# A new task order for a recurrent attention block with a gelu MLP behind it

## The chip, the cores and the metric

The kernel runs on one core of a Trainium2 chip. A core has five engines that run their own instruction lists and wait for each other by semaphores: TensorE (PE, matrix products into PSUM), VectorE (DVE), ScalarE (ACT), GpSimd (POOL) and SyncE (SP), which here does nothing but issue DMA transfers. The metric is the device time of one execution in microseconds (us).

## The reference

Two blocks follow each other, both in 32-bit floats. The first is a linear recurrence with a 40 by 40 state for each of 4 batches and 8 heads, over 768 steps:

```python
for t in range(S):
    y[:, :, t] = np.einsum('bhd,bhde->bhe', rt, state)
    Sa = np.einsum('bhde,bhe->bhd', state, at)
    state_decay = state * wt[:, :, None, :] - np.einsum('bhd,bhe->bhde', Sa, bt)
    state = state_decay + np.einsum('bhd,bhe->bhde', vt, kt)
```

The second takes the result as 3072 tokens of 320 numbers and runs them through an MLP of width 2048:

```python
h = x @ w_in
g = h * (1.0 / (1.0 + np.exp(-1.702 * h)))
return (g @ w_out).astype(np.float32)
```

## The kernel before, in words

The 768 steps are cut into 12 chunks of 64, and a chunk into two units of two batches each, so there are 24 units; unit i belongs to chunk i // 2 and needs the state that unit i - 2 left. Inside a unit the recurrence is written as products of 64 by 64 matrices for each head, and a triangular system that five "levels" of products invert. When both units of a chunk are done, the chunk's 256 tokens go through the MLP.

The work of a unit, by the names of its PSUM tiles and the lines of the code:

- `decay` (L536): the logarithms of w, their sums (`ps_cum`, `ps_cumc`; from unit 4 on a scan on DVE), and the exponentials FT, GT and G on ACT (L565 to L591).
- `prep` (L613): products of a, b and k with the exponentials (ahT L619, bhT L621, khT L624, kh and bh L627), the scores `ps_A` and `ps_RV` and their masks (L638, L650).
- `inverse` (L660): the score `ps_N`, its copies (P21 L692, E0 L689), then the levels. In the first four units a level is `ps_level` on PE, a copy of its result (PV, L784) and a transpose (EX, L723). In the others it is `ps_level`, a copy W (L751), a difference E (L753), a transpose ES (L702) and a spread over four diagonal blocks, EX (L707 on ACT, L709 on POOL or DVE). Then T0, Tc (L797), `ps_Q`, QT, `ps_T` and T (L830).
- `solve` (L835): the state read (`ps_zT`, `ps_rz`), the known part (`ps_B`, copies L891), the solution (`ps_X`, masked to M at L907), the result (`ps_y`), the new state (zraw, L934), the output read-out (L943) and its product with FT (x, L953). SP then writes x to DRAM (L963) and reads it back in another layout (xT, L967).
- `mlp` (L974): for a chunk 40 tasks "up" (`ps_up`, 64x256 products), four gelus on ACT (L988), and 16 tasks "down" (`ps_down`, 64x320 products), then a copy and an addition (L1012, L1014) and the store (L1011).

The weights come as eight pieces of four loads each, and each piece is then rebuilt from two words by ACT (L447), three DVE steps (L451 to L459) and POOL (L463). The first two pieces are needed by the first up, the fifth by the first down.

Nothing of this is scheduled when the kernel is built. `Plan.add` gathers 2700 tasks in a fixed sequence, with what each reads and which buffer must be free. `ORDER` is a text with one word per task: its number in that sequence, a letter for the engine (p PE, a ACT, d DVE, g POOL, s SP), and for tasks that touch PSUM a digit, which of the four pairs of PSUM banks the tile takes. `Plan.listed` reads the words, and the tasks are issued in that order; each engine thus takes its own tasks in the order of the text and waits, in place, for whatever a task needs:

```python
for one in text.split():
    e = next(e for e in ENGINES if ENGINES[e] in one)
    n, bank = one.split(ENGINES[e])
    t = self.tasks[int(n)]
    assert e in t.engines and t.after <= done and (e == "SP" or (t.pair is None) == (not bank))
    t.engine, t.bank = e, int(bank or 0)
```

`t.engines` names the engines on which a task may run: a W copy may be on ACT or DVE, a spread on ACT, DVE or POOL. Two tasks that read one PSUM pair on two engines take turns in the order of the text. SP is one such list as well: a load that waits for a free buffer holds up every transfer behind it.

Some numbers that come up again: 3a is the logarithm of unit 0; 103p and 159p are `ps_N` of units 0 and 1; 107, 110, 113, 116 and 119 are the levels of unit 0 (L0, L2, L4, L6, L8), 163, 166, 169, 172 and 175 those of unit 1 (L1, L3, L5, L7, L9); 292, 295, 298, 301, 304 and 362, 365, 368, 371, 374 the levels of units 2 and 3 (L10 to L19, even ones of unit 2); 136p and 192p are `ps_y` of units 0 and 1; 195 is x of unit 1 and 196s, 197s its way out to DRAM and back; 198p to 218p are the first ups; 19a is the first step of rebuilding weight piece 0; 2629p is `ps_y` of the last unit and 2634p the first up of the last chunk. In names like N(1) or M(0) the number is that of the unit.

Of the kernel before, what the change touches and what calls it, by code (L numbers as in the profile page):

```python
# [107 lines left out]
0s 8s 26s 5s 7s 9s 3a 6s 87p0 88p1 24s 89a1 1s 2s 12s 102a 95d 100p2 90a0 93d 158a 101d2 98p3 96g 10s 94d 17s 97g 16s 99d3  # L108
103p1 4a 11s 132p0 104a1 105d1 142p2 143p3 133a0 106d 130p1 14s 144a3 13s 107p0 15s 18s 151g 108a0 109d0 51s 131a1 110p3 27s
149g 150d 111a3 112d3 159p0 156p1 145a2 161d0 160a0 152g 113p3 345s 92a 162d 25s 153d 114a3 163p2 42s 115d3 34s 19a 274s 264p0  # L110
165d2 265p3 164a2 22d 266a3 166p2 20d 273s 21d 33s 43s 167a2 154p3 168d2 23g 35s 28a 157d1 116p2 155d3 169p1 117a2 118d2 267a0
279d 63s 280g 119p3 277s 171d1 36s 44s 123a3 120d3 343s 125d3 121a 278g 124d3 29d 287a 126p2 170a1 288p0 127a2 30d 172p1 479s
122a3 31d 289a0 128p2 54s 173a1 45s 129d2 32g 62s 174d1 134p3 37a 290d0 175p2 344s 135d3 180a2 146s 178a2 275s 176d2 136p1
179a2 38d 181a2 39d 177a 282g 276s 291d 91s 138a1 182p0 188p3 281d 183a0 186p2 139d 137a1 283p0 187a2 184p1 189a3 40d 140s
292p2 46a 60s 284d0 41g 285p3 185d1 148a 286d3 190p0 293a2 294d2 334p1 335p3 357a 191d0 141s 268g 147s 336a3 315d 192p2 47d
337a1 348d 316p0 194a2 346s 295p3 349d 61s 317a0 195g 347s 358p1 296a3 297d3 360d1 318a0 298p3 271a 361d 319p0 338g 300d3 196s
193a2 320a0 355p2 385d 270s 48d 299a3 362p0 356d2 351g 301p3 363a0 364d0 350g 386p2 197s 302d3 365p0 387a2 269s 352g 359a1
303d3 388a2 323p1 367d0 366a0 321p3 49d 324a1 304p2 322a3 478s 325d1 50g 353p0 309a2 470p3 354d0 209p1 307a2 210p1 310a2 305d2
211p1 308a2 272d 198p0 341a 199p0 72s 212p1 70s 64a 200p0 340s 368p2 52s 342d 339s 69s 201p0 369a2 202p0 370d2 203p0 471a
213p1 65d 214p1 389p2 66d 472a3 483g 204p0 390a2 560s 371p3 67d 306a 53s 215p1 71s 482s 216p1 372a3 217p1 476a 220p2 373d3 68g  # L120
218p1 221p2 477d 219a1 205p0 222p2 206p0 223p2 224p2 78s 559s 207p0 55a 311p3 225p2 79s 312d3 80s 226p2 208a0 58d 313p1 374p3
314d1 227p2 56d 379a3 228p2 229p2 57d 326p0 230a2 59g 393p1 327d0 378a3 391p2 394a1 375d3 231p0 558s 392d2 376a 232p0 233p0
395d1 81s 73a 234p0 480s 381p2 235p0 474s 328p1 475s 382a2 74d 377a3 485d 380a3 236p0 75d 481s 492a 242p2 486d 243p2 82a 76d
484d 77g 383p3 237p0 384d3 244p2 329d1 330d1 488p3 473d 238p0 531d 245p2 487g 246p2 489d3 85d 532p1 708s 239p0 533a1 396p3
331d 534a1 240p0 247p2 397d3 332s 241a0 562s 535p1 83d 490p3 536a1 84d 398p0 706s 572a 491d3 86g 550p1 253p3 399d0 551a 555s
400d0 561s 333s 254p3 401d 255p3 552a1 564d 493p0 402s 556a 567g 570p1 554s 494d0 248p2 705s 563d 566g 249p2 495d0 498d 256p3
571d1 565g 403s 250a2 496a0 251d2 696p1 497g 557d 539p0 252s 537p2 257p3 538a2 704s 540d0 701s 258p3 553d 611d 697a 499d 573p2
259p3 576a2 574d2 784s 710d 700s 260p3 787s 541d0 575d2 404p0 578d 261a3 577g 405p0 579d 698a1 568p2 711g 500p1 406p0 569d2
501a1 407p0 262d3 580p2 702a 502d1 263s 408p0 582d2 409p0 503d 410p0 583d 504a 612p3 411p0 584g 613d3 412p0 614d3 413p0 505p1
709d 414a0 426p3 506d1 427p3 428p3 507d1 429p3 699d 581d2 430p3 615p1 703d 431p3 616a1 785s 585p0 432p3 508d 586a0 433p3 587d0  # L130
434p3 509a 588d 435p3 589d 448p2 436a3 510p1 590p0 511a1 449p2 592d0 591a0 512d1 415p3 513d 416p3 593d 514a 417p3 594g 418p3
515p0 419p3 516a0 517d0 595p1 518d 420p3 596a1 597d1 421p3 598d 422p3 519a 599d 423p3 424p3 520p0 425a3 437p1 521d0 438p1
523d0 522g 439p1 524d0 440p1 525d0 441p1 442p1 526d0 527p3 718p0 528a3 443p1 719d0 929s 444p1 720d0 529p3 445p1 721d0 446p1
530d3 600p0 723d 447a1 542p3 722d 724g 603d0 605a0 619p1 604d0 543d3 450p2 620a1 606d0 544p3 621d1 601d0 602d 617p1 707s 546d3
451p2 618a1 783s 712d 547g 713d 607p0 725p1 608a0 452p2 609p0 453p2 548s 610d0 932s 454p2 727d1 726d1 622p0 728d 545d3 729a
775p1 455p2 623d0 780s 776a 549s 756d 730p3 624p0 456d2 457d2 731d3 458s 459p2 777a1 778g 732d3 786s 788g 781a 779s 626d0
460p2 625d0 627g 733d 795p1 835d 734a 461p2 735p3 791g 462p2 628s 736a3 796d1 737d3 716p0 792g 738d 463p2 782d 739g 1011s
920p1 757p3 925s 464p2 717d0 758a3 629s 759a3 790d 465p2 740p0 789d 466p2 741a0 742d0 921a 797p3 467d2 760p0 1008s 468d2 800a3
923d 652p2 469s 761d0 922a1 653p2 926a 930s 798d3 714p1 799d3 654p2 924s 802d 801g 655p2 934d 803a 656p2 836p0 657p2 715d1
658p2 659p2 837d0 762p3 838d0 927d 660p2 763a3 661p2 764p1 662a2 743d 630p0 744d 928s 631p0 632p0 765d1 804p3 766d1 633p0  # L140
805a3 806d3 634p0 807d 635p0 808a 745p2 636p0 748d2 637p0 749d2 839p1 933g 750d2 638p0 840a1 1009s 751d2 639p0 809p3 746d2
935g 640a0 641p1 810d3 642p1 793p2 747a 811d3 674p0 812d 794d2 813a 752p3 643p1 753a3 814p2 644p1 815a2 816d2 754p3 645p1
755d3 646p1 817d 647p1 818a 767p2 841p3 768d2 648p1 842a3 649p1 819p2 650p1 820a2 821d2 769p3 822d 651a1 823d 675p0 771d3 931s
770d3 772g 824p2 936d 676p0 827a2 828a2 942p1 829a2 677p0 1153s 830a2 937d 945a1 773s 663p3 825d2 664p3 943d1 1156s 826a 665p3
944d1 999p2 947d 946g 666p3 1000a 1004s 980d 940p1 948g 667p3 941d1 668p3 774s 669p3 670p3 831p1 671p3 1001a2 1002d 1003s
832d1 672p3 1005a 1013d 678p0 673a3 1006d 833p2 843p1 679p0 834d2 1007s 844d1 938p2 845d1 680p0 939d2 846p3 681p0 847d3 949p1
1012g 682d0 848p2 950a1 683d0 1014d 684s 685p3 849d2 1015g 1010s 850d2 1021p0 1016g 951d1 686p3 1024a0 1232s 851d 1235s 981p2
687p3 982a2 952d 852s 1022d0 983a2 953g 1144p1 1023d0 688p3 1026d 1145a 1149s 1025d 1027g 984p2 1059d 689p3 1154s 954p0 853s
985a2 1147g 690p3 1158d 1148s 955a0 956d0 986p2 1146a1 957d 1150a 691p3 958d 987a2 1151d 988p0 692p3 989a0 1152s 990d0 959p1
693a3 865p2 960a1 694d3 866p2 961d1 867p2 695s 962d 868p2 963d 1028p0 869p2 1029a0 1030d0 870p2 1031d 1157g 871p2 1159d 1032a  # L150
1060p3 872p2 873p2 1061a3 874p2 1062d3 1033p1 875a2 854p0 1035d1 855p0 1036d 856p0 1037d 1063p3 857p0 1064d3 1034a1 858p0
964p2 859p0 965a2 966d2 1038p1 967d 860p0 1039a1 1040d1 861p0 1041d 1017p3 968a 1042g 862p0 1018d3 863p0 969p2 864a0 876p1
970d2 877p1 972d2 971g 1043p3 973d2 878p1 1044a3 974d2 879p1 975d2 880p1 881p1 1045d3 1019p0 1046d 976p2 1047a 882p1 1020d0
1233s 883p1 977a2 1166p3 884p1 1169a3 1167d3 1377s 978p0 885p1 1168d3 898p2 1171d 1170g 886a1 979d0 887p3 1172a 1048p0 991p1
1051a0 888p3 1052a0 992d1 889p3 1053a0 890p3 1054a0 891p3 1049d0 993p1 1050a 1067p0 994d1 1160g 1155s 892p3 1161d 1068a0 893p3
894p3 1069d0 1380s 895p3 1204d 1065p0 995d1 896p3 996d 1066a0 1231s 1055p1 899p2 897a3 1056d1 997s 1173p0 1223p3 900p2 1174a0
1175d0 1228s 1176d 1224a 1177g 1057p1 901p2 1058d1 1070p0 998s 1164p1 1225a3 1226d 1236g 1227s 1071d0 902p2 1229a 1165d1
1162p3 903p2 1238d 1163d3 904p2 1237d 1178p0 1230d 905p2 1179a0 1180d0 1245p1 906a2 1181d 1072p3 1248a1 1456s 907d2 1182g
1246d1 908s 1247d1 909p0 1250d 1234s 1239g 1073d3 1251a 910p0 1240g 1074d3 1249d 1183p2 1459s 1283d 1368p1 911p0 1184a2 1075d
1373s 912p0 1185d2 1369a 1076s 1186d 1252p3 1187d 913p0 1370a1 1371g 1372s 1382d 1253a3 1188p2 1254d3 1374a 914p0 1255d 1190d2  # L160
1256g 1077s 1189a2 1191d 1243p1 1375d 915p0 1192g 1257p3 916p0 1244d1 1258a3 1259d3 1205p2 917d0 1206a2 1193p1 918d0 1207a2
# [968 lines left out]
```

## Time and profile before

| | |
|---|---|
| median of three runs | 679.86 us (679.8, 679.86, 681.62) |
| span of the profiled execution | 681.1 us |
| PE busy | 652.0 us (96%) |
| DVE busy | 445.5 us (65%) |
| ACT busy | 330.7 us (49%) |
| POOL busy | 176.7 us (26%) |
| `ps_up` matmuls | 254.4 us busy, 31% of the chain that ended last |
| `ps_down` matmuls | 240.3 us busy, 30% of that chain |
| `ps_level` matmuls | 9% of that chain |
| moved by DMA | 69.73 MB, 102 GB/s over the span |

The times of the three runs are of whole executions; the span is that of the one execution that the hardware profiler recorded, from its first instruction to its last. In a row such as `L751 ACT COPY W<-ps_level 128x512 f32 x56 | 32.7, 585 | 69.1 <-PE ...` one reads: line, engine, operation, output and input with their shapes, how many; busy time in us and the mean of one in ns; the idle time just before them and what ended it. A matmul of 32-bit floats appears twice in the records, and four of them run side by side on quarters of the array, so a matmul's own duration is much longer than the interval at which they follow each other. PEclk is the granted clock of TensorE as a share of full speed.

### The profile page before, as it was taken

How to read it: one execution, taken by the hardware profiler on the slowest of the kernel's cores; microseconds unless marked ns; L12 is line 12 of the kernel's file. 1: busy time of each engine (PE TensorE's matmuls, PEld its weight loads, DVE VectorE, ACT ScalarE, POOL GpSimd, SP SyncE). 2: the span in 40 equal slices, each digit the busy share in tenths (PEclk: the TensorE clock that was granted, in tenths of full speed). 3: DMA queues.
4: the chain of work that ended last, by engine and by line, in shares of the span. 5: the costliest groups of instructions: out<-in, count | busy, mean ns of one | idle time of the engine just before them, and what ended most of it. 6: DMA issues, size and time to landing. Idle time of an engine off the chain costs nothing.

```text
span 681.1 us, 42181 instructions
## 1 busy us (share of the span) xinstructions
PE 652.0 (96%) x19488; PEld 572.4 (84%) x19488; DVE 445.5 (65%) x906; ACT 330.7 (49%) x688; POOL 176.7 (26%) x204
## 2 busy tenths in 40 slices
PE   5777999999999999999999999999999999999997
PEld 5667888997987788888888898899899799889996
DVE  4687877777867668767776587868556766675001
ACT  4675845544564654664545445455454354252110
POOL 5443444225123123123123211321412421300000
PEclk9788999999999999999999999999999999999999
DMA  7874755205314314432404413513502312200100
GB/s 235 275 244 148 228 158 173 89 14 155 108 50 139 103 45 125 124 108 67 121 23 131 140 34 107 154 33 106 149 29 71 121 51 58 58 13 23 51 12 21
DMA packets 35312, 69.73 MB, mean 102 GB/s; under 512 B 5440, under 2 KB 14656, under 8 KB 35136
## 3 DMA queue, kind: packets, MB, share of 16 engines
q1 hardware_dynamic: 35136, 67.03, 32.8%
q8 instruction: 153, 2.51, 1.6%
q14 instruction: 23, 0.19, 0.1%
HBM read 59.15 MB, written 7.86 MB: 98 GB/s over the span
## 4 chain that ended last, share of the span: by engine, by line
PE 91%; DMA 4%; ACT 1%; DVE 1%; issue 1%; SPq 0%; ACTq 0%; DVEq 0%
PE ps_up L300 31%; PE ps_down L300 30%; PE ps_level L300 9%; PE ps_y L300 5%; PE ps_B L300 4%; PE ps_X L300 2%; PE ps_N L300 2%; PE ps_rz L300 2%; PE ps_RV L300 2%; PE ps_A L300 1%; DMA ak<-in_ak 1%; PE ps_zT L300 1%; PE ps_Q L300 1%; DMA time<-in_time 1%; PE ps_T L300 1%
## 5 line engine op out<-in xcount | busy, mean ns | idle before, releaser
L300 PE MATMUL ps_up<-xT_all,w_sb 64*64 64x256 f32 x3840 | 254.4, 377 | 2.0 <-DMA xT_all<-x_dram 1.1
L300 PE MATMUL ps_down<-w_sb,g 64*64 64x320 f32 x3072 | 240.3, 430 | 1.1 <-issue 0.9
L300 PEld LDWEIGHTS ps_up<-xT_all,w_sb 64*64 64x64 f32 x3840 | 172.9, 133 | 17.7 <-issue 2.5
L300 PEld LDWEIGHTS ps_down<-w_sb,g 64*64 64x64 f32 x3072 | 143.3, 133 | 31.4 <-issue 1.6
L988 ACT ACTIVATE g<-ps_up 128x1024 f32<-128x1024 f32 x48 | 49.1, 1024 | 44.7 <-PE ps_up L300 44.3
L709 POOL TENSOR_TENSOR EX<-ES,quads 128x512 f32<-128x512 f32 x29 | 38.3, 1323 | 115.5 <-DVE ES L702 83.1
L751 ACT COPY W<-ps_level 128x512 f32<-128x512 f32 x56 | 32.7, 585 | 69.1 <-PE ps_level L300 67.4
L300 PEld LDWEIGHTS ps_level<-W,EX 64*64 64x64 f32 x2560 | 59.2, 134 | 5.8 <-DVE T L830 0.2
L300 PE MATMUL ps_level<-W,EX 64*64 64x64 f32 (+1 forms) x2560 | 56.2, 217 | 0.0
L753 DVE TENSOR_TENSOR E<-two,ps_level 128x256 f32<-128x256 f32 x80 | 33.1, 415 | 34.7 <-ACT W L751 30.7
L707 ACT ACTIVATE EX<-ES,quads 128x256 f32<-128x256 f32 x80 | 36.3, 501 | 30.4 <-DVE ES L702 29.9
L619 POOL TENSOR_TENSOR ak<-ak,FT 128x512 f32<-128x512 f32 x16 | 22.0, 1378 | 76.2 <-DMA ak<-in_ak 54.4
L300 PE MATMUL ps_level<-PT,EX 64*64 64x64 f32 (+2 forms) x1280 | 34.9, 244 | 5.7 <-DVE EX L723 4.8
L300 PEld LDWEIGHTS ps_level<-PT,EX 64*64 64x64 f32 x1280 | 32.6, 145 | 8.9 <-DVE EX L723 5.7
L702 DVE STREAM_TRANSPOSE ES<-E 128x256 f32<-128x256 f32 x80 | 35.2, 442 | 4.7 <-DVE E L753 0.5
L300 PE MATMUL ps_y<-M,bh 64*64 64x104 f32 (+1 forms) x768 | 34.8, 247 | 1.3 <-DVE M L907 0.8
L300 PE MATMUL ps_y<-RV,kh 64*64 64x104 f32 (+1 forms) x768 | 34.9, 247 | 0.3 <-DVE EX L723 0.3
L891 ACT COPY B<-ps_B 128x416 f32<-128x416 f32 (+1 forms) x34 | 16.5, 492 | 33.5 <-PE ps_B L300 33.2
L300 PEld LDWEIGHTS ps_y<-RV,kh 64*64 64x64 f32 x768 | 28.9, 133 | 2.0 <-DVE M L907 0.5
L907 DVE TENSOR_TENSOR M<-ps_X,later 128x832 f32<-128x832 f32 (+1 forms) x24 | 23.8, 993 | 9.8 <-PE ps_X L300 9.5
L627 POOL TENSOR_TENSOR kh<-time,G 128x320 f32<-128x320 f32 x18 | 16.2, 902 | 48.4 <-PE ps_y L300 34.4
L300 PEld LDWEIGHTS ps_y<-M,bh 64*64 64x64 f32 x768 | 27.0, 133 | 1.9 <-DVE M L907 1.2
(131 smaller groups left out, 1097.2 us busy)
## 6 DMA issues: line engine op xcount, KB each, us to landing
ak<-in_ak SPq DMA_DIRECT2D x48, 160.0 KB
rv<-in_rv SPq DMA_DIRECT2D x48, 160.0 KB
time<-in_time SPq DMA_DIRECT2D x24, 320.0 KB
xT_all<-x_dram SPq DMA_DIRECT2D x48, 160.0 KB
wc<-in_wc SPq DMA_DIRECT2D x20, 264.0 KB
logw<-in_w SPq DMA_DIRECT2D x24, 160.0 KB
RV<-in_v SPq DMA_DIRECT2D x24, 160.0 KB
b<-in_b SPq DMA_DIRECT2D x48, 80.0 KB
```

Source lines behind the costliest of these rows:

```text
L300: nc.tensor.matmul(o, lhsT, rhs, start=start, stop=True, skip_group_check=True)
L619: plan.add(R, {"DVE": 690.0, "POOL": 1270.0, "sbuf": True}, lambda t: of(t.engine).tensor_mul(ahT(), ahT(), FT_of(i)), reads=T("ak", "FT") ...
L627: plan.add(R + 4, {"POOL": 870.0, "DVE": 490.0, "sbuf": True}, lambda t, n=n, dst=dst: of(t.engine).tensor_mul(dst(i)[:, :, :D], by_head(t ...
L702: plan.add(rank, dve(256), lambda t: nc.vector.transpose(ES(n), source(t)), writes=[key("ES", n, 6)], **reads)
L707: nc.scalar.activation(dst[:, :, h], ES(n), ACT.Copy, scale=quads[:, h, :1])
L709: of(t.engine).tensor_mul(dst, ES(n).unsqueeze(2).to_broadcast([128, 8, 2, 32]), quads.unsqueeze(1).to_broadcast([128, 8, 2, 32]))
L751: plan.add(rank, any2(512), lambda t: copy(t.engine)(tiles_of(W(n + 1)), blocks(psum(t, ""), 64)), writes=[key("W", n + 1, 5)], pair=pair)
L753: plan.add(rank, dve(256), lambda t: nc.vector.tensor_sub(tiles_of(E(n + 1)), every(two32, [128, 2, 4, 32]), blocks(psum(t, ""), 64)[:, :, ...
L891: plan.add(R, any2(4 * wide), lambda t: copy(t.engine)(dst(), some(psum(t, "")[:, :, :208])), writes=[("Bv", i)] if x and c > 0 else T("B" ...
L907: plan.add(R + 1, dve(8 * wide), lambda t: nc.vector.tensor_tensor(M_of(i)[:, :, :wide].rearrange("p (j b) n -> p b j n", b=2), some(psum( ...
L988: plan.add(-45, {"ACT": 1030.0, "table": "gelu"}, lambda t: nc.scalar.activation(g_of(c * NQ + q).rearrange("p m r n -> p r m n"), psum(t, ...
```

## The change

The text `ORDER` is replaced by another; nothing else in the kernel differs. All 2700 tasks are there as before, and each does the same arithmetic. The new text was found by a search on an estimate that lets the packets that bring the instructions queue behind the loads on the DMA engines. It changes three things: the order of the tasks on each engine, the engine of the tasks that have a choice, and the PSUM pairs.

```diff
 ORDER = """
-0s 8s 26s 5s 7s 9s 3a 6s 87p0 88p1 24s 89a1 1s 2s 12s 102a 95d 100p2 90a0 93d 158a 101d2 98p3 96g 10s 94d 17s 97g 16s 99d3
-103p1 4a 11s 132p0 104a1 105d1 142p2 143p3 133a0 106d 130p1 14s 144a3 13s 107p0 15s 18s 151g 108a0 109d0 51s 131a1 110p3 27s
...
+0s 7s 26s 102a 1s 5s 11s 100p0 3a 88p1 158a 8s 6s 9s 4a 51s 87p2 89a1 12s 95d 93d 17s 94d 103p1 105d1 101d0 98p3 90a2 96g 97g
+10s 2s 143p2 16s 104a1 99d3 142p0 106d 13s 132p3 133d3 107p1 15s 144a2 24s 130p2 109d1 151g 131d2 108a1 92a 110p1 149g 150d
...
-2468p0 2630d2 2559s 2469p0 2631d 2470p0 2632s 2471p0 2475p1 2472a0 2473d0 2476p1 2474s 2633s 2477p1 2478p1 2479p1 2480p1
-2634p3 2635p3 2636p3 2637p3 2638p3 2639p3 2640p3 2641p3 2642p3 2643p3 2481p1 2644a3 2482p1 2645p2 2483a1 2646p2 2484d1 2678p0
...
+2475p2 2628d3 2476p2 2629p3 2630d3 2477p2 2474s 2478p2 2558s 2559s 2479p2 2480p2 2631d 2632s 2481p2 2482p2 2633s 2634p3 2645p1
+2635p3 2636p3 2637p3 2638p3 2646p1 2647p1 2648p1 2649p1 2639p3 2640p3 2641p3 2483d2 2484d2 2485s 2642p3 2643p3 2650p1 2651p1
...
 """
```

How many tasks with a choice stand on which engine (those with a change of three or more):

| task | before | after |
|---|---|---|
| W copy, L751 | ACT 56, DVE 24 | ACT 38, DVE 42 |
| EX spread, L707 and L709 | ACT 40, DVE 31, POOL 29 | ACT 34, DVE 44, POOL 22 |
| T0 spread | ACT 13, DVE 5, POOL 6 | ACT 9, DVE 12, POOL 3 |
| B copies, L891 | ACT 34, DVE 14 | ACT 21, DVE 27 |
| P21 copy, L692 | ACT 22, DVE 2 | ACT 12, DVE 12 |
| QT, L816 | ACT 18, DVE 6 | ACT 13, DVE 11 |
| Tc copy, L797 | ACT 44, DVE 52 | ACT 54, DVE 42 |
| kh, L627 | DVE 6, POOL 18 | DVE 11, POOL 13 |
| ahT, L619 | DVE 8, POOL 16 | DVE 11, POOL 13 |
| khT, L624 | DVE 12, POOL 12 | DVE 7, POOL 17 |
| wz, L595 | DVE 12, POOL 10 | DVE 7, POOL 15 |
| W0 difference, L697 | DVE 9, POOL 11 | DVE 12, POOL 8 |
| zT copy, L858 | ACT 25, DVE 19 | ACT 29, DVE 15 |
| last copy of the output, L1012 | ACT 15, DVE 9 | ACT 12, DVE 12 |

ACT switches between its exponential and its gelu table 25 times in the new text, 29 times in the old one. PE waits for semaphores in 237 instructions of their own, 293 before. Between `ps_y` of the last unit and the first up of the last chunk stand six downs of the chunk before, where there were ten.

More of the change, by code (lines that the diff above doesn't have):

```diff
@@ L243 @@
[L243 to L244 removed]
+0s 7s 26s 102a 1s 5s 11s 100p0 3a 88p1 158a 8s 6s 9s 4a 51s 87p2 89a1 12s 95d 93d 17s 94d 103p1 105d1 101d0 98p3 90a2 96g 97g
+10s 2s 143p2 16s 104a1 99d3 142p0 106d 13s 132p3 133d3 107p1 15s 144a2 24s 130p2 109d1 151g 131d2 108a1 92a 110p1 149g 150d
+159p2 112d1 111a1 156p3 14s 145a0 161d2 162d 160d2 113p1 115d1 114d1 163p0 164a0 153g 265p2 152d 264p1 18s 19a 165d0 20d 266a2
@@ new lines @@
+2122g 2139p2 2179d 2076d0 2146d 1972s 1973s 2265a 2278d 2269s 2124s 1809p1 1810p1 1811p1 2145d 2147g 2075d0 2140d2 2106p2
+2268s 2148p0 2267g 2266a3 2270a 2149a0 2271d 1974p3 1975p3 1976p3 1977p3 1978p3 2107a2 1979p3 2150d0 2077d 2108p2 1980p3
+2180p0 2181a0 2078g 2182a0 1981p3 2109d2 2151d 2152d 1982p3 2272s 1983p3 2137p0 1812p1 2110d2 2138d0 1985p2 2353s 1813d1
+2153p0 1986p2 1984a3 1987p2 1814d1 2154d0 2079p1 2155d0 2156d 2080d1 2183p3 2157d 2184a3 2351s 2277g 1988p2 2081d1 2082d
+2018p0 1989p2 2158p1 2083d 1990p2 1991p2 2160d1 2279g 2161d 2084p3 1992p2 2085a3 2159d1 1993p2 2086d3 2087d 1994p2 1996p1
@@ new lines @@
+2038d2 2209p2 2303p0 2304d0 2305d0 2496d 2210p2 2370p1 2211p2 2039s 2201p3 2306d 2307d 2372d1 2212p2 2373d 2202p3 2203p3
+2204p3 2374a 2308p0 2310d0 2205p3 2309a0 2489d 2206p3 2371d1 2207p3 2213p2 2311d 2359p1 2375p0 2312g 2208a3 2377d0 2376a0
+2378d 2379a 2360d1 2497d 2214p2 2215p2 2216p2 2217p2 2218p2 2220p1 2221p1 2380p0 2382d0 2222p1 2219a2 2383d 2223p1 2405p2
+2313p3 2406d2 2381a0 2384a 2224p1 2314d3 2225p1 2319a3 2566s 2226p1 2385p2 2227p1 2228p1 2387d2 2386d2 2315g 2320p0 2229p1
+2321d0 2504p2 2317d3 2230a1 2388d 2389g 2318d3 2316a3 2505d2 2507d2 2242p0 2243p0 2506d2 2231p2 2508g 2232p2 2322p3 2323d3
```

255 lines of the change are left out of this document (122 added, 133 removed).

## The prediction

> **What bounds the kernel now.** I read the page's busy line and its slices first, then busy time by stretch, then the PE intervals and the instruction queue's packets, then the chain of waits, last the operation groups.
>
> ```profile
> PE 652.0 (96%) x19488; PEld 572.4 (84%) x19488; DVE 445.5 (65%) x906; ACT 330.7 (49%) x688; POOL 176.7 (26%) x204
> PE   5777999999999999999999999999999999999997
> PEclk9788999999999999999999999999999999999999
> DMA  7874755205314314432404413513502312200100
> q8 instruction: 153, 2.51, 1.6%
> ```
>
> TensorE is busy everywhere but in the first six slices and the last. The next rows, busy time by stretch, show the head: DMA is 0.77 to 0.84 busy for 51 us, PE works 64 of the first 85 us, and its granted clock falls to 0.80.
>
> ```profile
> core 0: us, PE busy (x) PEld busy (x) DVE busy (x) ACT busy (x) POOL busy (x), PEclk, DMA share, GB/s
> 0.00:17.00 17.00, 9.48 (x248) 8.56 (x248) 7.90 (x14) 6.99 (x25) 9.91 (x42) 1.00 0.80 235
> 17.00:34.00 17.00, 12.10 (x412) 10.90 (x416) 10.86 (x16) 10.46 (x21) 8.03 (x6) 0.80 0.84 275
> 34.00:51.00 17.00, 12.53 (x489) 11.25 (x486) 14.26 (x28) 13.14 (x33) 7.48 (x4) 0.90 0.77 244
> 51.00:68.00 17.00, 13.24 (x542) 12.16 (x532) 12.44 (x18) 9.71 (x25) 6.47 (x11) 0.90 0.49 149
> 85.00:102.00 17.00, 15.60 (x414) 13.76 (x408) 12.12 (x23) 7.85 (x18) 7.12 (x3) 1.00 0.52 159
> ```
>
> Busy time of overlapping matmuls hides short waits, so I took, for every PE task, the interval to the next task's first matmul, and each kind's median (up 0.432 us, down 1.077, y 1.427, a solver level 0.465, or 1.10 with W beside it). The medians of all 1080 tasks sum to 640.9 us. First task 3.75, last task starts 674.83: so 30.2 us are waits, 26.6 before 102 us and 3.6 after; 6.3 us follow (last down, store). Work does not change, so the new order can move only these waits. The first up starts at 69.0 us after 40.9 us of work: 28.1 us lost there.
>
> Some waits belong to the instruction stream. 39272 PE instructions came in 153 packets of 16384 bytes, one per 256 instructions. At each 256th, the next packet is requested (its start follows by a median 0.68 us, 2 to 3 us under loads, and it takes 0.88 to 1.76), and PE does not pass the following boundary until 1.3 to 1.5 us after the landing, wherever it stands still there. The chain of waits shows it as "issue":
>
> ```profile
> 54.25 0.56 issue
> 58.98 0.85 issue
> 70.94 0.19 issue
> 89.77 0.48 issue
> 95.04 0.92 issue
> ```
>
> At these boundaries PE's instructions stood still for 0.76, 1.06, 0.57, 0.86 and 1.34 us; later for 0.70 (196 us), 0.43 (557) and 0.28 (611). With one at 67 us (0.29) that is 6.3 us.
>
> **The change.** It moves every task, so I cost it by stage. The price rows of moved work:
>
> ```profile
> L751 DVE COPY W<-ps_level 128x512 f32<-128x512 f32 x24 | 16.3, 681 | 7.9 <-PE ps_level L300 7.6
> L751 ACT COPY W<-ps_level 128x512 f32<-128x512 f32 x56 | 32.7, 585 | 69.1 <-PE ps_level L300 67.4
> L709 DVE TENSOR_TENSOR EX<-ES,quads 128x512 f32<-128x512 f32 x31 | 21.7, 699 | 1.0
> L707 ACT ACTIVATE EX<-ES,quads 128x256 f32<-128x256 f32 x80 | 36.3, 501 | 30.4 <-DVE ES L702 29.9
> ```
>
> Task counts by these durations: DVE from 452 to 492 us (18 W copies at 0.68, 13 spreads at 0.70, B, P21, T0 copies), ACT 342 to 306 (four table loads at 1.28 fewer among it), POOL 163 to 146. Beside 641 us of PE work all three stay hidden on average. Where not, it shows in one of four terms.
>
> *Head, to the first up.* I followed the new lists by hand: each engine takes its tasks in order, a task begins 0.05 us after its last input or predecessor, two engines reading one PSUM pair take turns in list order (as L723 waits for L784's copy now), loads land by their place in SP's queue at the measured 0.27 MB/us. Before in brackets. ak(1) has 3.44 MB up to it (3.11), so lands near 17.9 (16.7); b(1) is early; both POOL products follow (1.38, 1.28) and N(1) starts 20.5 (20.67). Unit 0's lead of half a microsecond is lost behind N(1) on PE: L4 22.3 (22.46), L3 27.65 (27.80). Then weight 0's rebase (1.40) stands behind unit 1's level copy on ACT, not before it: L5 31.45 (31.56). L7 comes at 35.55 (37.61), since DVE takes EX7 before three masks and bhT(2). M(0) 40.65 (41.71). Unit 1's last transpose goes ahead of the Tc copies, so its T0 spread starts 42.15 (44.57); T(1) 46.95 (49.02); M(1) 49.15 (51.44); y(1) ends 51.9 (53.78). x(1) on POOL runs 52.75 to 54.7; 2.5 us out and 3.4 back make xT 60.6. Meanwhile L11 58.6 (61.27), L16 60.75 (63.03), L13 62.35 (64.92), and the first up, whose xT then waits already, at 63.2 (69.0). SP blocks twice, at RV(2) until y(0) and at RV(3) until y(1); what is queued behind, ak(3) and xT(0)'s first half, has 7 us to spare. PE has 38.7 us of work before the first up (40.9). So waits fall from 28.1 to 24.5: -3.6. The other bound: DVE has 48.6 us before the first up (45.0). If it is the limit, the first up comes 3.6 later, 2.2 less work done: +5.8. I take -2.8, near the walk, a quarter off for packet waits that it leaves out (block 9 of the stream, 256 instructions, now holds 1.78 us of work, the least of all).
>
> *Packets from the first up to 102 us.* 2.8 us lost now. A block must hold the wait for the packet, its transfer and 1.4: 3.2 to 5.7 us. Blocks 13 to 18 hold 4.1 to 4.7 each (3.8 to 5.9), beside 5.0 MB of loads (5.8), the heaviest 1.5 MB (1.75). Between -2.8 and +1: -1.3, the middle, as neither end has a nearer row.
>
> The Trainium skill, page "Runtime: NRT & Kernel Launch", section "Instruction fetch mechanics", says that the sequencer fetches the next page while executing the current one and that crossing a 16 KiB boundary is "mostly hidden". The trace agrees on the packet (256 instructions) and not on the cost (6.3 us here); by the rule this term would be 0.
>
> *102 to 660 us.* 3.6 us of waits now, 1.5 of it at 491 us where xT of chunk 8 came late. Between y of a chunk's second unit and its first up lie 10.9 to 16.5 us of PE work (12.0 to 15.0); out-and-back took 8.6 to 14 us before. Chunks 2 and 8 are shortest, 11.1 and 10.9: +0.4 each, and the old 1.5 goes. Blocks of under 3.2 us of work: four, 0.7 us short in all (three, 0.2): +0.5. DVE's share over 20 us of PE work reaches 0.89 (0.76): +1.0, between 0 and 6. Level hops keep their cover: the tightest reserve is 0.2 us in both. Sum +0.8.
>
> *The end.* After y(23) only six downs cover x(23)'s way out and back, 6.46 us (ten, 10.8). The quiet way is read-out 0.7, products 0.9, out 2.2, back 3.2, 0.3 between: 7.3. So +0.8; at worst +2.5, if a store holds SP as the one at 634 us did. The last copy on ACT gives 0.06.
>
> Sum: -2.8 - 1.3 + 0.8 + 0.8 = -2.5, on the profile's span of 681.1: 678.6. The runs were 679.8, 679.86 and 681.62; the median is 1.2 below the span, so I say 677.4.
>
> **Rivals.** *The walk comes true whole*: -3.6, packets -2.8, no loss at DVE: about 673. For it: DVE idles 0.2 of the head even now. Against: ideal hops. Chance 0.22. *DVE sets the head* (slower): place, 20 us to the first up; price +5.8 for -2.8, so 686; it decides when DVE is busy over 0.9 of that stretch (0.84 from 34 to 51 now). Chance 0.13. *DVE's dense stretches break the cover* after 102 us: +6 for +1, 682.4; for it the 0.89, against it 65% now without one level wait. Chance 0.12. *The order does not do what it says*: loads and packets still collide, the packet term is 0 and the walk gives half: about 679.5, no change that can be told. Chance 0.19. My sum's case, 675 to 679: 0.34.
>
> By the Trainium skill's page named above packets cost nothing, and the change would give the rest of the sum alone, 678.7. The five "issue" rows speak against the rule; it lies inside the fourth rival's chance.
>
> **How the numbers follow.** Less than 0.3%, 2.0 us, can hardly be told from none. Faster: 0.22 and most of 0.34, 0.55; same 0.20; slower 0.25. The range leaves out the far ends of the first two rivals: 672 to 684.5; the sum's own is 675 to 679.
>
> **What would show it.** First up near 63 to 65 us; y(1) ending near 52; less "issue" in the chain between 54 and 102 us; a new PE wait of about 1 us for xT near 630 to 640. DVE busy near 486 us, ACT near 300. I am wrong if the first up comes after 69 us, if PE waits on DVE through the middle stretches, or if packets still stop PE by 6 us.

## The result and the profile after

The new kernel takes 707.04 us (median of four runs, 705.63 to 707.95), the old one 679.83 beside it: 1.0415 times as long, 95% interval 1.0381 to 1.0449. The forecast was 677.4, in a range of 672 to 684.5. The profiled execution has a span of 706.2 us (681.1 before). Times here and below are medians of all executions of a kernel; the ratios and intervals leave out those in the chip's slower state.

First the page: the busy line, the 40 slices of PE, of its granted clock and of the DMA engines, and the instruction queue.

```profile
PE 660.6 (94%) x19488; PEld 544.7 (77%) x19488; DVE 474.4 (67%) x960; ACT 293.2 (42%) x630; POOL 156.4 (22%) x189
PE   4678899999999999999999999999999999999897
PEclk9989999999999999999999999999999999999999
DMA  8946623503314413422404413412412411200200
q8 instruction: 153, 2.51, 1.4%
```

The page looks almost as before: nines everywhere, more work on DVE, less on ACT. The 4% are lost in waits too short for a slice. Busy time by stretch shows the head:

```profile
core 0: us, PE busy (x) PEld busy (x) DVE busy (x) ACT busy (x) POOL busy (x), PEclk, DMA share, GB/s
0.00:17.00 17.00, 8.15 (x220) 7.17 (x224) 8.33 (x15) 6.49 (x23) 8.60 (x42) 1.00 0.82 243
17.00:34.00 17.00, 11.03 (x452) 9.27 (x444) 14.11 (x20) 9.42 (x21) 7.86 (x6) 1.00 0.95 327
34.00:51.00 17.00, 11.88 (x432) 11.00 (x432) 13.65 (x23) 10.07 (x28) 6.68 (x7) 0.80 0.41 120
51.00:68.00 17.00, 13.67 (x524) 11.73 (x524) 15.36 (x23) 8.38 (x21) 11.95 (x10) 1.00 0.66 207
...
85.00:102.00 17.00, 15.61 (x460) 12.09 (x456) 15.62 (x24) 9.90 (x16) 6.92 (x4) 1.00 0.33 114
```

The loads are pulled forward: DMA is 0.95 busy from 17 to 34 us (0.84 before) and 0.41 in the next stretch (0.77). The two longest pieces of "issue" that the chain of waits has between 30 and 130 us are longer than any before:

```profile
36.72 2.01 issue
...
72.26 1.91 issue
```

The copies and spreads kept their durations to 0.02 us and changed only their counts, as reckoned:

```profile
L709 DVE TENSOR_TENSOR EX<-ES,quads 128x512 f32<-128x512 f32 x44 | 31.3, 715 | 0.8
L707 ACT ACTIVATE EX<-ES,quads 128x256 f32<-128x256 f32 x68 | 30.8, 501 | 38.8 <-DVE ES L702 35.4 <-PE ps_y L300 3.2
...
L751 DVE COPY W<-ps_level 128x512 f32<-128x512 f32 x42 | 28.4, 677 | 9.8 <-PE ps_level L300 9.7
L751 ACT COPY W<-ps_level 128x512 f32<-128x512 f32 x38 | 22.1, 584 | 55.4 <-DVE E L753 29.6 <-PE ps_level L300 25.7
```

So PE's work is the same (its medians differ by 1.3 us in sum), and the time went into waits. The view of what PE waited for between 102 and 640 us (line, what it waited for, us in total, times, longest) has four lines before:

```profile
PE ps_up L300 <- DMA xT_all<-x_dram: 1.1, 1, 1.1
PE ps_y L300 <- issue: 0.5, 1, 0.5
PE ps_down L300 <- ACT zr L869: 0.2, 1, 0.2
PE ps_up L300 <- PE ps_rz L300: 0.2, 1, 0.2
```

Now its first are:

```profile
PE ps_up L300 <- DMA xT_all<-x_dram: 2.0, 3, 1.1
PE ps_zT L300 <- DVE ob L1014: 1.4, 1, 1.4
PE ps_up L300 <- issue: 1.0, 2, 0.6
PE ps_B L300 <- DVE ob L1014: 0.9, 1, 0.9
PE ps_B L300 <- issue: 0.8, 1, 0.8
PE ps_y L300 <- issue: 0.7, 1, 0.7
PE ps_level L300 <- POOL EX L709: 0.7, 1, 0.7
```

To see all of them I took again, task by task, what the interval to PE's next task has above its kind's median, and gave each excess of 0.08 us or more after 102 us to what ended last before it: a packet boundary, a reader that freed the PSUM pair or wrote the operand, or xT (slow ups behind such a wait included).

| after 102 us, us | packets | pairs and results | xT | rest | sum |
|---|---|---|---|---|---|
| before | 1.6 | 1.6 | 3.5 | 0.5 | 7.2 |
| after | 7.6 | 9.7 | 10.1 | 1.8 | 29.1 |

(Of the 3.5 us for xT before, 1.7 are the wait at 491 us itself, which is what the expectations below count.) The difference, 21.9 us, is nearly the whole loss. Both texts have issued exactly the same tasks after their 590th and after their 2371st word, so the traces can be compared there without any median: PE goes on at 145.4 and 152.1 us (+6.6), at 564.6 and 584.3 (+19.7), and the last task ends 25.2 us later. The loss sits in head, middle and tail.

### The profile page after: what moved, and what is told of

It reads as the page before. It is cut to its first block, busy times and chain, and to the rows that moved or that the text cites. A ratio compares the mean times of both kernels' runs of the same rounds, so it can differ in the third digit from the quotient of the medians.

```text
span 706.2 us, 42068 instructions
## 1 busy us (share of the span) xinstructions
PE 660.6 (94%) x19488; PEld 544.7 (77%) x19488; DVE 474.4 (67%) x960; ACT 293.2 (42%) x630; POOL 156.4 (22%) x189
## 4 chain that ended last, share of the span: by engine, by line
PE 76%; DMA 10%; DVE 7%; issue 4%; SPq 2%; ACT 1%; POOL 1%; DVEq 0%; POOLq 0%; ACTq 0%
PE ps_up L300 28%; PE ps_down L300 22%; PE ps_level L300 8%; PE ps_y L300 4%; PE ps_B L300 4%; DMA x_dram<-x 2%; PE ps_X L300 2%; DMA ak<-in_ak 2%; DMA b<-in_b 1%; PE ps_A L300 1%; DMA xT_all<-x_dram 1%; PE ps_N L300 1%; PE ps_rz L300 1%; PE ps_zT L300 1%; PE ps_Q L300 1%
## 5 line engine op out<-in xcount | busy, mean ns | idle before, releaser
L300 PEld LDWEIGHTS ps_up<-xT_all,w_sb 64*64 64x64 f32 x3840 | 166.3, 135 | 38.2 <-issue 13.0
L300 PEld LDWEIGHTS ps_down<-w_sb,g 64*64 64x64 f32 x3072 | 133.5, 133 | 44.8 <-issue 2.2
L709 POOL TENSOR_TENSOR EX<-ES,quads 128x512 f32<-128x512 f32 x22 | 30.0, 1365 | 119.2 <-DVE ES L702 107.4
L707 ACT ACTIVATE EX<-ES,quads 128x256 f32<-128x256 f32 x68 | 30.8, 501 | 38.8 <-DVE ES L702 35.4
L751 ACT COPY W<-ps_level 128x512 f32<-128x512 f32 x38 | 22.1, 584 | 55.4 <-DVE E L753 29.6
L624 POOL TENSOR_TENSOR ak<-ak,GT 128x512 f32<-128x512 f32 x17 | 22.2, 1308 | 93.1 <-DMA ak<-in_ak 30.0
L1014 DVE TENSOR_TENSOR ob<-ob,ps_down 128x320 f32<-128x320 f32 x24 | 11.5, 481 | 39.9 <-ACT ob L1012 39.6
L797 ACT COPY Tc<-ps_level 32x64 f32<-32x64 f32 x108 | 21.8, 202 | 35.9 <-DVE ES L702 12.6
L751 DVE COPY W<-ps_level 128x512 f32<-128x512 f32 x42 | 28.4, 677 | 9.8 <-PE ps_level L300 9.7
L709 DVE TENSOR_TENSOR EX<-ES,quads 128x512 f32<-128x512 f32 x44 | 31.3, 715 | 0.8
```

The source lines that it names most:

```text
L300: nc.tensor.matmul(o, lhsT, rhs, start=start, stop=True, skip_group_check=True)
L624: plan.add(R, {"DVE": 690.0, "POOL": 1270.0, "sbuf": True}, lambda t: of(t.engine).tensor_mul(khT(), khT(), GT_of(i)), reads=T("ak", "GT") ...
L707: nc.scalar.activation(dst[:, :, h], ES(n), ACT.Copy, scale=quads[:, h, :1])
L709: of(t.engine).tensor_mul(dst, ES(n).unsqueeze(2).to_broadcast([128, 8, 2, 32]), quads.unsqueeze(1).to_broadcast([128, 8, 2, 32]))
L751: plan.add(rank, any2(512), lambda t: copy(t.engine)(tiles_of(W(n + 1)), blocks(psum(t, ""), 64)), writes=[key("W", n + 1, 5)], pair=pair)
L797: copy(t.engine)(dst, src[:, u, :, f])
```

## Experiments: where the loss sits

*The stretches one by one.* Since the sets agree at the two cuts, a text may begin in one order and go on in the other. In each of three runs one stretch is new and the rest old (where two orders meet, the PSUM pairs of the later one are renamed to fit).

```diff
-0s 8s 26s 5s 7s 9s 3a 6s 87p0 88p1 24s 89a1 1s 2s
+0s 7s 26s 102a 1s 5s 11s 100p0 3a 88p1 158a 8s 6s 9s
...
 443p2 719d3 929s 444p2 720d3 529p1 445p2 721d3 446p2 530d1
```

> The first 590 tasks (to about 150 us) in the new order, on the new engines and pairs, the other 2110 as in the old kernel. Both orders have done exactly the same tasks at this cut; the traces put 6.6 us of the loss ahead of it. Theory S (each stretch loses by itself, from how its own tasks stand): 685 to 688. Rival C (the head puts loads and engines out of step, and that is carried into the rest): 690 or more.

```diff
 442p1 526d0 527p3 718p0 528a3
-443p1 719d0 929s 444p1 720d0 529p3 445p1 721d0 446p1 530d3
+719d0 529p3 443p1 444p1 530d3 720d0 445p1 600p3 721d0 542p0
...
```

> The tasks 590 to 2371 (about 145 to 565 us) in the new order, the head and the tail as in the old kernel. The traces put 13.1 us of the loss here. Theory S: 691 to 695. Rival C: without the new head the middle loses at most half of it, 684 to 688.

```diff
 2229p0 2242p1 2507a2 2505d2 2230a0
-2506d2 2509d 2508g 2231p3 2510a 2322p2 2390p0 2323d2
+2243p1 2506d2 2231p2 2508g 2232p2 2322p3 2323d3 2390p0
...
```

> The last 329 tasks (from about 565 us) in the new order, all else as in the old kernel. The traces put 5.4 us here, most of it the wait for x of the last unit behind six downs and the half clock after it. Theory S: 684 to 687. If that wait came from what the new kernel had ahead of it in SP's and POOL's lists, 680 to 682.

Measured: head 690.92 us (1.014, 1.0104 to 1.0175), middle 700.23 (1.0277, 1.0226 to 1.0327), tail 686.26 (1.0077, 1.0044 to 1.0111), the old kernel beside them 680.88. The three sum to 1.049; the new kernel itself, run again on another chip, took 715.56 us, 1.0497 (1.0431 to 1.0562). So each stretch loses by itself (theory S), and the middle's 19 us do not come from the head. By their times alone only the tail lies where theory S had it; the head's run is in rival C's range, and the middle lost more than either said. The traces decide: the run with the new head is 8.0 us late at the first cut (153.4 us for 145.4) and 5.1 us at the end, so nothing is carried on; the run with the new middle takes 433.2 us from cut to cut for 419.2 and loses 0.6 us behind the second cut. The head and the middle cost more than the first traces had put there (9.6 and 19 us for 6.6 and 13.1): on these chips the new order is slower than in the first comparison.

> The new kernel unchanged, on the same chip as the three others, to measure the first of them against: 705 to 713 by the runs so far.

*Engines.* Each text with the other's engines, 315 letters changed:

```diff
-106d 13s 132p3 133d3 107p1 15s 144a2 24s 130p2 109d1 151g 131d2
+106d 13s 132p3 133a3 107p1 15s 144a2 24s 130p2 109d1 151g 131a2
```

> The new order and the new PSUM pairs, with every task back on the engine that it had before (315 tasks differ). Theory D: the new kernel loses its time because DVE carries 27 to 40 us more work and is late in reading PSUM pairs (after 102 us PE waits 8.4 us for a pair to be read, nearly all for DVE; before, 1.6). Then those waits shrink to about 2 us, some 3 us more come back in the head, and the time is 696 to 700. Rival P: the loss is the instruction packets (11.3 us of stalls for 6.4), which follow the order of PE's own tasks, and that stays: 705 to 709. Rival F: order and engines were chosen for each other, and the mixture is worse than either: over 709.

> The old order and the old PSUM pairs, with the new engine of every task. Theory D: DVE's longer list alone brings waits of PE for PSUM pairs, 6 to 9 us, so 686 to 689. Rival P: packets follow PE's order, which is the old one, so 679 to 682. Rival F: worse than D says, over 690, since the old order places DVE's tasks for the old choice.

New order on old engines 735.6 us (1.0764, 1.0705 to 1.0822), old order on new engines 700.69 (1.0271, 1.023 to 1.0312). Theory D falls: putting DVE's extra work back makes the new order slower still. Both mixtures lose, each text's order is fitted to its engines (rival F), and an engine letter has no price of its own apart from the order.

*PSUM pairs.* 170 of 476 tiles of the new kernel enter a pair that was read less than 0.5 us before, 75 in the old one. I gave the new order, where it leaves a choice, the pair that was free longest (101 tight tiles then remain), and the old order pairs as tight as the new one's:

```diff
-93d 17s 94d 103p1 105d1 101d0 98p3 90a2 96g 97g
+93d 17s 94d 103p3 105d3 101d0 98p1 90a2 96g 97g
```

> The new order on the new engines, but each PSUM tile takes, of the pairs that the order leaves it, the one that was read out first in the new kernel's trace (355 of 480 tiles change their pair). In the old kernel 75 of 476 tiles are written less than 0.5 us after their pair was last read, in the new one 170; with this choice it would be 101. Theory R: the new kernel's pairs leave no reserve, and PE waits wherever a reader is a little late. Then waits for pairs after 102 us fall from 8.4 us to 3 to 4, 1 to 2 us come back in the head, and the time is 699 to 703. Rival O: it is the order, which holds more tiles at once (three others live at 189 of 391 tile starts between 102 and 640 us, 115 before); the choice of the pair only moves the wait to the next tile: 705 to 710.

```diff
-12s 102a 95d 100p2 90a0 93d 158a 101d2 98p3 96g
+12s 102a 95d 100p1 90a0 93d 158a 101d1 98p0 96g
```

> The old order on the old engines, but each PSUM tile takes the pair that was read out last, if that was at least 0.15 us before it starts in the old kernel's trace: 167 of 476 tiles then come less than 0.5 us behind the last reader, about as many as in the new kernel. Theory R: reserve by itself is worth 6 to 10 us: 686 to 690, with waits for pairs after 102 us of 6 to 10 us for 1.6. Rival O: with the old order's short lives of the tiles nothing is late by more than the reserve: 680 to 684.

The free pairs gave 712.21 us (1.0453, 1.0402 to 1.0505): nothing gained, with 10.4 us of waits for pairs and results after 102 us. The tight pairs cost 1.0061 (1.0032 to 1.009), and not there: those waits are 1.6 us as in the old kernel, the packets 4.9 for 1.6. So theory R falls, though the second time lies between what R and O said: 167 tiles that enter a pair less than 0.5 us after its last reader cost the old order nothing in waits for pairs, since its readers are on time. In the new order readers are late, and other pairs do not help.

## Experiments: why readers are late

Following each wait for a reader back along that reader's engine, I found it most often behind a row of prep work. The longest in the first half (1.36 us of PE at 118.7) as DVE's timeline has it: start, duration, line and operation, in brackets the idle time and what ended it.

```profile
116.41 0.49 DVE L627 TENSOR_TENSOR kh<-time,G 128x320 f32<-128x320 f32 x1 [1.69 <-DMA time<-in_time]
116.82 1.37 DVE L533 TENSOR_TENSOR_SCAN wc<-starts,wc 128x264 f32<-128x264 f32 x1
118.11 1.70 DVE L534 TENSOR_TENSOR_SCAN wc<-starts,wc 128x264 f32<-128x264 f32 x1
119.74 0.46 DVE L845 TENSOR_TENSOR zr<-zraw,wz 128x320 f32<-128x320 f32 x1
120.12 0.47 DVE L1014 TENSOR_TENSOR ob<-ob,ps_down 128x320 f32<-128x320 f32 x1
```

DVE stands 1.69 us for a load, then works through the prep of later units; the addition that frees the pair of the finished down is last, and `ps_B` waits for it. In the next run ten such tasks, and no others, stand earlier in DVE's list (only DVE's words are shown here):

```diff
-564d 571d2 553d 566d 557d 611d 251d1 495d3
+251d1 564d 571d2 553d 566d 557d 611d 495d3
```

> The new kernel with ten tasks of DVE moved ahead in its list: reads of a PSUM pair (or results) that PE was seen waiting for, moved past tasks in front of them that nobody needed for at least as long as the move delays them (the addition of the first output past six, the read-out of y(4) past a spread, zraw(13) past three and so on). They released 5.1 us of PE's waits between 102 and 640 us. Theory Q: PE waits for a pair because an urgent read stands in DVE's list behind prep work that is not urgent; then 3 to 5 us are gone against the new kernel on this chip. Rival T: every place is tight, and as much comes back at the next task: within 1.5 us of the new kernel.

707.62 us against 715.56 for the new kernel on the same chip (1.0388, 1.0334 to 1.0442, against 1.0497, 1.0431 to 1.0562; the intervals overlap by a hair). Waits for pairs and results after 102 us are 5.6 us for 11.6 in the new kernel's trace of the same job. That is theory Q, in ten places: 8 us between the medians, 4.8 between the spans of the two profiled executions (706.8 and 711.6), for 3 to 5 expected. In the profiled execution of the edited kernel the packets' stops after 102 us are 2 us longer than in the new kernel's.

What a late transfer does in place showed most plainly where the old kernel got the new text's order of transfers and nothing else (only SP's words are shown here):

```diff
-0s 8s 26s 5s 7s 9s 6s 24s 1s 2s 12s 10s 17s 16s 11s
+0s 7s 26s 1s 5s 11s 8s 6s 9s 51s 12s 17s 10s 2s 16s
```

> The old kernel in everything but SP's list: its transfers are issued in the new kernel's order, up to the last of the first 2371 tasks (197 of 268 stand in another place). Theory L: this list sets which loads the instruction packets and x meet; packet stops rise from 6.4 us to 9 to 11 and x comes later in places, so 683 to 686. Rival N: when a transfer runs is set by the buffer that it waits for, not by its place in the list: 679 to 682.

717.24 us (1.051, 1.0459 to 1.0562): neither theory. The view of what PE waited for, and DVE's timeline:

```profile
PE ps_up L300 <- DVE B L894: 7.3, 1, 7.3
```

```profile
136.41 0.69 DVE L621 SCALAR_TENSOR_TENSOR b<-b,GT 128x512 f32<-128x512 f32 x1 [7.30 <-DMA b<-in_b]
```

One load of b, now behind a transfer of xT in SP's list, lands late; DVE stands at its prep task for 7.3 us; the sum of B that is next in its list can't free its pair; PE waits as long. A place in SP's list thus has a price of several us, through two lists that it does not stand in. This wait is a fifth of that run's loss of 36 us; its packets stop PE for 18 us (6.6 before), and one copy of B, late on ACT, costs another 4.4 us. What each of the 197 moved transfers costs is not shown. The new kernel's own lists avoid this one, and have smaller ones of the kind (the 1.69 us above).

## Experiments: the tail

> The new kernel up to its last 72 tasks, and these in the old order, on the old engines (so ten downs again between the last y and the first up of the last chunk). The traces put 4.2 us of the loss behind this cut. If it is the six-down cover and the half clock after the 3.25 us wait, that comes back whole: 702 to 704. If x of the last unit comes late for another reason (what lies ahead of it in POOL's or SP's list), the wait returns in another place and 705 to 707 remain.

This gave 712.29 us (1.0461, 1.0398 to 1.0524): nothing came back, PE's wait for x of the last unit was 4.54 us. The edit did not do what the expectation says. The cut lies behind the store discussed below and behind the downs that the new text issues ahead of y, and the old order of the rest puts two of the remaining six downs behind the first ups: four downs stood between y and the first up, not ten. The run says nothing about a cover of ten. Then the downs alone, in the old kernel:

```diff
-2467p0 2629p2 2468p0 2630d2 2559s 2469p0 2631d 2470p0 2632s 2471p0 2475p1
+2467p0 2468p0 2469p0 2470p0 2471p0 2629p2 2630d2 2559s 2631d 2632s 2475p1
```

> The old kernel with four of the ten downs that stand between y of the last unit and the first up of the last chunk moved ahead of that y, all else the same. In the old kernel's trace x needs 7.96 us from the end of y to the landing, and PE goes on 1.9 us after a landing that it waits for, 9.8 in all, against 6.46 us of six downs. Theory S: a wait of 3.3 us and 2 us more at the half clock behind it: 685 to 687. By the prediction's term (0.8 us): 680.5 to 682.

683.53 us for 682.24 (1.001, 0.9973 to 1.0047): the prediction's term. The last packet of xT is in 6.6 us after the end of y here, where that took 9.3 in the old trace, so six downs (6.46 us) nearly cover it: PE waits 0.23 us and goes on 0.1 us after that packet. (The expectation's 7.96 us reach only to about the first packets of xT, and its 1.9 us are mostly the others.) The way was longer in the old kernel because a store of output stood ahead of the way back and waited until 634.1 us for DVE's addition; with the downs moved, the addition is done earlier. In the new kernel x of unit 23 is not even computed before 2.5 us after y, and the list of transfers says why (start, duration, engine and line):

```profile
652.74 1.11 SPq L1011 DMA_DIRECT2D out<-ob  x2
653.89 0.89 SPq L963 DMA_DIRECT2D x_dram<-x  x2
657.48 1.12 SPq L967 DMA_DIRECT2D xT_all<-x_dram  x2
658.69 0.83 SPq L963 DMA_DIRECT2D x_dram<-x  x2
```

x of unit 22 was ready at 651.8, but the store of output 20 stands ahead of its way out and waits for DVE's addition until 652.7. There is one x buffer: x of unit 23 can be written only when unit 22's has left it at 657.4. The store was moved, in the kernel with the new tail:

```diff
-2476p2 2629p3 2630d3 2477p2 2474s 2478p2 2558s 2559s 2479p2 2480p2 2631d 2632s 2481p2
+2476p2 2629p3 2630d3 2477p2 2478p2 2558s 2559s 2479p2 2480p2 2631d 2632s 2474s 2481p2
```

> The old kernel with the new tail, as in the experiment of the new tail, but one transfer stands three places later in SP's list: the store of output 20, behind x(23)'s way out and no longer ahead of x(22)'s. Theory X: x(22) goes out about 2 us sooner, the one x buffer is free sooner, the product of x(23) starts 1 to 1.3 us after y instead of 2.7 to 3.0, PE's wait of 3 to 4.4 us shrinks to 1 to 2 and most of the half clock behind it goes: 1.002 to 1.004 of the old kernel instead of 1.008. Rival: x(22)'s way out waits for its own product, and nothing changes: 1.007 to 1.010.

683.95 us for 681.95: 1.0016 (0.9989 to 1.0043) for 1.0077 with the store where the new text has it. One word of 2700 carries 0.6%, some 4 us, most of the tail's loss; the two intervals, from two chips, do not overlap. How much of it shows differs by execution: in the new kernel's second trace, with the store in the same place, PE waited 1.7 us for x of the last unit (3.1 in the first), and the tail behind 2371 words lost 2.8 us for 5.5. The chain of waits through the new tail (the kernel of the third stretch run):

```profile
637.23 0.51 SPq L963
637.74 0.04 issue
637.78 3.24 DMA x_dram<-x
...
642.81 3.10 DMA x_dram<-x
645.91 0.02 SPq L967
645.94 0.03 issue
645.97 2.90 DMA xT_all<-x_dram
```

and with the store moved, where it no longer leaves PE but for 0.90 us:

```profile
633.65 6.46 PE ps_down L300 x96
640.11 0.90 issue
641.01 10.70 PE ps_up L300 x189
```

## Experiments: the instruction packets

A stop is counted here where PE stands at a packet boundary and resumes within 1.8 us of the packet's landing. (The expectations used 1.6, which left out the two longest stops of the new kernel: they say 11.3 us where this count has 15.9.) Over the whole kernel: 6.6 us before; 15.9 and 17.5 in the new kernel's two traces. The packet for the stop at 72 us was requested at 67.5 and began at 71.6. The DMA engines in that window:

```profile
DMA  9999999899999999999999989998779898999999
...
DMA packets 1170, 2.41 MB, mean 345 GB/s; under 512 B 127, under 2 KB 255, under 8 KB 1169
...
q8 instruction: 1, 0.02, 0.8%
```

One packet of 16 KB among 2.4 MB of loads. Of all 153 packets 35 waited over 1.5 us from request to start, 19 before. What the loads make of this:

```diff
-            rows = [slice(p.start, p.start + D) for p in HALF] if name in ("ak", "b", "rv") else [slice(0, 128)]
+            rows = [slice(p.start, p.start + (D if i < 4 else 1)) for p in HALF] if name in ("ak", "b", "rv") else [slice(0, 128)]
```

> The new kernel with the loads of ak, b and rv cut to one row of each half from unit 4 on (26 of 69.7 MB less; the data are then old ones, and the two exponentials behind FT and GT are taken of zero so that nothing grows; the number of instructions is the same). Theory L: after 102 us the instruction packets wait behind these loads (24 of 130 wait over 1.5 us from request to start, 10 before), and that makes 7.6 us of stops for 1.6 and lengthens x's way. Then stops fall under 2 us, waits for xT by 1 to 2, and the time is 697 to 701. Rival B: the stops come from blocks with too little PE work, whatever the loads do: stops stay at 6 to 8 us, 704 to 708.

> The old kernel with the same loads cut. Theory L: it has 1.6 us of packet stops and 1.7 of waits for xT after 102 us to lose, so 677 to 680; the distance of the two kernels falls from 25 to 28 us to 19 to 22. Rival B: the distance stays 25 to 28 us.

702.09 us (1.0292, 1.022 to 1.0365) and 679.45 (0.9981, 0.9949 to 1.0012). The new order gains 1.2 to 2% by the lighter loads, the old one 0.2%: the distance falls to 22.6 us. After 102 us the new order has 3.9 us at packets (7.6), 7.2 for pairs and results (9.7) and 7.2 for xT (10.1). So the loads act through all three, as theory L has it for two of them, but less than it said (stops under 2 us, 697 to 701 us, a distance of 19 to 22). They account for a sixth to a third of the distance (27 us in the first comparison, 33 in the last; the new kernel itself was not run on this chip).

Do the stops depend on where the boundaries happen to fall? My first try added 64 matmuls to the new kernel's first `ps_N`:

```diff
+            for _, (e, b) in product(range(16 if i == 0 else 0), QUARTERS):
+                mm(ps[HALF[b], e, :64], ident[HALF[e]], ident[HALF[e]], True)
```

> The new kernel with 64 small matmuls more in the task of the first score N, in which PE waits 3.9 us anyway: 128 PE instructions, half a packet, so that every packet boundary falls half a packet from where it fell, in front of the same work. Theory P1: whether a boundary stops PE is the accident of which work lies behind it; then the new stops are other ones, and their sum is 7 to 13 us for 11.3, the time 704 to 709. Theory P2: the stops belong to places with dense small tasks or many loads, wherever the boundary falls exactly, and sum and time stay within 1 us of 11.3 and 707. If the task itself is delayed by the matmuls the time is up by at most 1.5 us.

I had miscounted: a matmul of 32-bit floats leaves two records and two weight loads, so 64 of them are 256 instructions, a whole packet, and every boundary stays in front of the same work. The time, 714.4 us (1.0394, 1.0297 to 1.049), is the new kernel's; the run tells nothing about the place. With `range(8 ...)` it is half a packet, first in the old kernel, then in the new one:

> The old kernel with 32 small matmuls (64 records, 128 instructions) more ahead of the first score N, in which PE waits 1.5 us anyway: the packet boundaries fall half a packet from where they fell. Theory P1 (accident): the old kernel's 6.4 us of stops, 1.6 of them after 102 us, belong to a lucky place of the boundaries; shifted, the stops are 9 to 13 us and the time 683 to 687. Theory P2 (places with dense small tasks and loads): stops 5.5 to 8 us, 679.5 to 682.5.

> The new kernel with the same 32 small matmuls as in the half-packet run of the old one. If the stops are set by where the boundaries fall, they move to other places and their sum leaves the 11 to 18 us of the new kernel's runs, up or down by 4 us or more; the old kernel sat in a lucky place, the new one in an ordinary one, so most likely 13 to 22 us and 708 to 718. If the sum stays within 11 to 18 us and the time within 705 to 716, the place of the boundaries is nothing special in the new kernel, as an ordinary place should be.

The old kernel takes 690.35 us for 682.24 (1.0133, 1.0087 to 1.0179), with 23.6 us of stops. Nothing but 128 instructions was added. In this trace they did not fall wholly into a wait: the first score N started 1.7 us after the first of them, so up to 1.7 us may be their own time, though a stop of 3.0 us follows at once. The chain of waits between 5 and 102 us now has these pieces among others:

```profile
14.69 3.00 issue
...
59.17 1.63 issue
...
63.70 1.69 issue
...
72.23 1.40 issue
```

The new kernel takes 717.46 (1.0495, 1.0443 to 1.0548), as unshifted on another chip (1.0497). So P1 holds for the old kernel, and by more than it expected: its place of the boundaries is better than the one other place that was tried, by 6 to 12 us. In the new order moving the boundaries did not change the time, as far as two chips can be compared. Its trace, of the longest of its four executions, has some 23 us of stops, above the 11 to 18 that the expectation allows an ordinary place, so it stays open whether the new kernel's place is ordinary. Stops differ by execution too: four traces whose stream is the old one up to 565 us have 6.5, 7.5, 10.8 and 11.2 us of them until then, the shifted one 22.8. The 6.6 us of the first trace are thus the least of four. That the estimate behind the new order took the packets into account does not show in these traces.

## Why the prediction was wrong

- **102 to 660 us: +0.8 forecast, about +18 came.** This is the step that failed. Of its parts, blocks "under 3.2 us" looked at PE's work only: the new blocks are no shorter (median 4.31 us from boundary to boundary, 4.10 before), but more packets start late. "DVE's share" was taken as a price of +1.0, at most +6; waits for readers rose by 8.1 us at 67% DVE. It is not DVE's extra work as such: with that work put back on ACT and POOL the new order took 735.6 us. A share over 20 us does not see a list that stands still for a load, nor which of its tasks is urgent. And "level hops keep their cover" asked only of levels, not of output additions, sums of B, zraw and y that free pairs, which are where PE mostly waited. The runs show in place of this step: late readers (ten reads moved ahead give back 5 to 8 us) and late packets and xT behind bunched loads (lighter loads give back 5 to 11).
- **Head: -2.8 forecast, -0.2 came.** The walk held, or the kernel was ahead of it, to 35 us (N(1) 20.38 for 20.5, L4 22.13 for 22.3, L5 30.36 for 31.45, L7 34.72 for 35.55). Then a packet requested at 31.36 landed at 37.09, PE stood 2.2 us, and everything behind is late: the spread of T0(1) 44.24 for 42.15, y(1) ends 54.57 for 51.9, the first up starts at 66.63 for 63 to 65 (69.01 before). Work before it is 38.7 us, as forecast. The walk had no packets in it, and "a quarter off" was too little.
- **First up to 102 us: -1.3 forecast, +3.0 came** (5.3 us lost for 2.3), 2.3 of it in the one stop at 72 us. Counting bytes ahead of a block does not say when they run: the loads were bunched. The term itself was also mis-added: the middle of -2.8 and +1 is -0.9, not -1.3, and the 2.8 us that it starts from are three stops, while the intervals of this stretch have only 2.3 us lost in all.
- **The end: +0.8 forecast, "at worst +2.5 if a store holds SP"; +4.2 came.** The price of the six downs fits (1.001, 0.9973 to 1.0047). The store was the mechanism and was priced too low: it delays not only a transfer but, by the single x buffer, the product of the next unit, and PE ran its first ups behind the wait at half clock (0.86 us for 0.43).
- **The sizes of the moved work were right**: DVE 474 us (486 forecast), ACT 293 (300), PE's work unchanged. The first up came earlier in the first trace, but not in the new kernel's second one (69.75 us). Of the signs of being wrong two came: packets stop PE by more than 6 us, and PE waits on DVE through the middle stretches. One reading of the rows was off: PE's slices are under 9 in the first four, not six.
- **Rivals.** None reached 690. DVE's dense stretches, the nearest in kind, was priced at +6 and has 8.1; the packet rival allowed no gain, and stops rose by 9.3 us. Both came together with the tail. The Trainium skill, page "Runtime: NRT & Kernel Launch", section "Instruction fetch mechanics", has the crossing "mostly hidden". By count the traces agree: PE stops at 11 of some 150 boundaries in the old kernel, at 28 with the shift. But "mostly" was read as "costs nothing" in the prediction, and those few cost 6.6 and 23.6 us.

Left open: what the remaining waits for pairs (about 5 us with ten reads moved) and the head's other waits are, one by one; no run took them away. Nor did any mixture of the two orders beat the old kernel.

## What to carry to other kernels

A hand-written or searched order has no price for one word: an urgent read, a load or a store is paid for by what stands behind it in its engine's list, so follow every list past each place where it can stand still for a transfer, and ask which task behind it frees a buffer. Where instructions are fetched in packets, compare two orders with the boundaries in more than one place; a kernel that was picked among many runs may owe some of its time to where they fall (that the old one was picked so is not shown). An estimate that has loads, packets and queues in it still needs reserve in each of them.

## What the runs showed of the hardware

- 128 more PE instructions ahead of the first score cost the old kernel 1.3% (6.6 us of stops became 23.6) and the new one nothing that can be told (1.0495 for 1.0497). A packet of 16 KB waited 4.7 us for its start at 31 us and 4.2 us at 67 us, there among loads that keep the DMA engines 98% busy; PE resumed 1.2 to 1.7 us after a landing that it waited for.
- One and the same kernel took 705 to 720 us (the new one, on two chips) or 676 to 688 (the old one, over all its runs).
- After a PE wait of 3.1 us in the tail, five of the next six ups came every 0.82 to 0.86 us instead of 0.43. After a wait of 1.7 us, in the new kernel's second trace, only the first interval was longer, and the granted clock stayed at 1.00. The first trace's stretch shows the clock behind its wait:

```profile
660.00:664.00 4.00, 1.46 (x24) 0.55 (x16) 0.98 (x2) 0.00 (x0) 0.00 (x0) 1.00 0.40 131
664.00:668.00 4.00, 3.47 (x38) 2.55 (x42) 0.00 (x0) 0.00 (x0) 0.00 (x0) 0.72 0.19 47
668.00:672.00 4.00, 4.00 (x70) 3.25 (x66) 0.00 (x0) 0.00 (x0) 0.00 (x0) 0.85 0.00 0
```
